# Linear attention regrouped around one matrix, phi read from PSUM by ScalarE alone, and transposes by DMA on the crossbar, in a four-layer attention and gated-MLP kernel

## The chip, the cores and the metric

The kernel runs on one core of one Trainium2 chip; the three later sessions used three chips. The metric is device time in microseconds (us) of one execution. Every execution told here was fast, with a granted TensorE clock of at least 0.99 of full speed as the mean of a run. A ratio is the mean time of one kernel's fast runs over the mean of the other's in the same rounds, so it is not quite the ratio of the medians quoted beside it.

Engine names: PE is TensorE, PEld its weight loads, DVE VectorE, ACT ScalarE, POOL GpSimd, and SP the engine that issues the DMAs.

## The reference

There are four layers: attention, MLP, attention, MLP. Each adds its result to `x`, which is 2048 x 1024, and normalises its input first.

```python
def _A_ref(x, wqkv, wo):                 # H = 32 heads of 32
    q, k, v = split(x @ wqkv)
    phi = lambda t: jnp.where(t > 0, t + 1, jnp.exp(t)) + 1e-6
    pq, pk = phi(q), phi(k)
    kv  = jnp.einsum("bhsd,bhse->bhde", pk, v)
    z   = jnp.einsum("bhsd->bhd", pk)
    num = jnp.einsum("bhqd,bhde->bhqe", pq, kv)
    den = jnp.einsum("bhqd,bhd->bhq", pq, z)[..., None] + 1e-6
    return merge_heads(num / den) @ wo
def _B_ref(x, w_gate, w_up, w_down):     # F = 3584
    return ((x @ w_gate) * (x @ w_up)) @ w_down
```

## The kernel before

The parts that matter, with cuts marked:

```python
def transpose_tile(src, dst):                    # 128 x 1024, on TensorE
    pt = psum.tile([P, KD, P], BF16, tag="tr", bufs=1, name="pt")
    for k in range(KD):
        nc.tensor.transpose(out=pt[:, k, :], in_=src[:, k * P:(k + 1) * P], identity=ident[:])
    nc.scalar.copy(out=dst, in_=pt[:])

def phi(ps, dst):                                # 128 x 512; VectorE reads PSUM too
    e = eb[phis[0] % 3]
    ...
    nc.scalar.activation(out=e, in_=ps[:], func=ACT.Exp)
    nc.vector.tensor_scalar(out=e, in0=e, scalar1=1.0, scalar2=1e-6, op0=ALU.min, op1=ALU.add)
    nc.vector.scalar_tensor_tensor(out=dst, in0=ps[:], scalar=1.0 + 1e-6, in1=e, op0=ALU.add, op1=ALU.max)

def kv_unit(t):                                  # phi(k)' [v, ones], 128 x 132 blocks
    ...
        for c in range(KD):
            nc.tensor.matmul(out=acc[0][:, c, 0:ZW], lhsT=pk[t % 4][:, c * P:(c + 1) * P],
                             rhs=vz[t % 4][:, c, :], ...)

def o_unit(t):                                   # phi(q) [kv, z], then a division
    ...
        for c in range(KD):
            nc.tensor.matmul(out=ps[:, c, 0:ZW], lhsT=pqT[g % 3][:, c, tl * P:(tl + 1) * P],
                             rhs=KVz[:, c, :], start=True, stop=True)
    ...                                          # divide, transpose the result, multiply by wo
```

Each attention projects K, V and Q, accumulates `kv` over the 16 row tiles, divides, transposes each output tile and multiplies it by `wo`. Per attention K, V, Q and out take 256 matmuls of 512 columns each; `kv` and `o` take 128 of 132 columns each. Normalised tiles and attention outputs are transposed on TensorE through a single PSUM buffer, 96 tiles of eight 128-column matmuls in all.

Of the kernel before, what the change touches and what calls it, by code (L numbers as in the profile page):

```python
# [9 lines left out]
ALU = mybir.AluOpType  # L10
BF16 = mybir.dt.bfloat16
# [3 lines left out]
def weave(main, fill, first, step):  # L15

    out, fill = [], list(fill)
    for i, u in enumerate(main):
        out.append(u)
        if fill and i >= first and (i - first) % step == 0:  # L20
            out.append(fill.pop(0))
    return out + fill
# [3 lines left out]
def kernel(  # L26
# [23 lines left out]
    MM = 3  # L50
    HC = P // 32
    ZW = P + HC
    ZS = NB // 2
# [3 lines left out]
    work = ctx.enter_context(tc.tile_pool(name="work", bufs=4))  # L57
# [3 lines left out]

    X = const.tile([P, NT, D], BF16, tag="X", name="X")
    xT = [const.tile([P, KD, G], BF16, tag=f"xT{i}", name=f"xT{i}") for i in range(NG)]
    Wr = [const.tile([P, KD, NB], BF16, tag=f"W{i}", name=f"W{i}") for i in range(4)]
    Dr = [const.tile([P, 4 * D], BF16, tag=f"D{i}", name=f"D{i}") for i in range(KF // 4)]
    H = const.tile([P, KF * G], BF16, tag="H", name="H")
    KVz = const.tile([P, KD, ZW], BF16, tag="KVz", name="KVz")

    hT = H[:].rearrange("p (f s) -> p f s", s=G)
    pk = [H[:, i * D:(i + 1) * D] for i in range(4)]  # L70
    o0 = 4 * D
    vz = [H[:, o0 + i * KD * ZW:o0 + (i + 1) * KD * ZW].rearrange("p (c f) -> p c f", f=ZW) for i in range(4)]
    o0 += 4 * KD * ZW
    onat = [H[:, o0 + i * D:o0 + (i + 1) * D] for i in range(4)]
    o0 += 4 * D
    eb = [H[:, o0 + i * NB:o0 + (i + 1) * NB] for i in range(3)]
    oT = [H[:, i * KD * G:(i + 1) * KD * G].rearrange("p (c s) -> p c s", s=G) for i in range(2)]
    wk = Wr[0:2]
    wv = Wr[2:4]
    wo = [Dr[i][:].rearrange("p (k n) -> p k n", n=NB) for i in (0, 1)]  # L80
    pqT = [Dr[i][:].rearrange("p (c s) -> p c s", s=G) for i in (2, 3, 4)]
    wq = [Dr[i][:].rearrange("p (k n) -> p k n", n=NB) for i in (5, 6)]
    wd = [Dr[f // 4][:, (f % 4) * D:(f % 4 + 1) * D] for f in range(KF)]
    ring = [Wr[0], Wr[1], Wr[2], Wr[3], xT[2], xT[3]]
# [9 lines left out]

    def load(dst, src):
        nc.sync.dma_start(out=dst, in_=src)

    def load_k(n):
        load(wk[n][:], wqkv_v[:, :, D + n * NB:D + (n + 1) * NB])

    def load_v(n):
        load(wv[n][:], wqkv_v[:, :, 2 * D + n * NB:2 * D + (n + 1) * NB])

    def load_q():
        for n in range(2):
            load(wq[n], wqkv_v[:, :, n * NB:(n + 1) * NB])

    def load_o():
        for n in range(2):
            load(wo[n], wo_v[:, :, n * NB:(n + 1) * NB])  # L110

    def load_gu(i):
        fb = i % FB
        load(ring[2 * i % 6][:], wg_v[:, :, fb * NB:(fb + 1) * NB])
        load(ring[(2 * i + 1) % 6][:], wu_v[:, :, fb * NB:(fb + 1) * NB])

    def load_d():
        for i in range(KF // 4):
            load(Dr[i][:].rearrange("p (f n) -> p f n", n=D), wd_v[:, 4 * i:4 * i + 4, :])

    load(X[:, 0, :], x_view[:, 0, :])
    load(X[:, 1, :], x_view[:, 1, :])
    for k in range(0, KD, 4):
        load(wk[0][:, k:k + 4, :], wqkv_v[:, k:k + 4, D:D + NB])
    load(X[:, 2, :], x_view[:, 2, :])
    load(X[:, 3, :], x_view[:, 3, :])
    load_k(1)
    load_v(0)
    load_v(1)
    for t in range(TPG, 2 * TPG):  # L130
        load(X[:, t, :], x_view[:, t, :])
    load_q()
    for t in range(2 * TPG, NT):
        load(X[:, t, :], x_view[:, t, :])
    load_o()


    ident = const.tile([P, P], BF16, tag="ident", name="ident")
    make_identity(nc, ident[:])
    mask = const.tile([P, ZW], F32, tag="mask", name="mask")  # L140
    nc.gpsimd.memset(mask[:], 0.0)
    for b in range(HC):
        nc.gpsimd.memset(mask[32 * b:32 * b + 32, 32 * b:32 * b + 32], 1.0)
        nc.gpsimd.memset(mask[32 * b:32 * b + 32, P + b:P + b + 1], 1.0)
    mhalf = const.tile([P, 1], F32, tag="mhalf", name="mhalf")
    nc.gpsimd.memset(mhalf[:], -0.5)
    warm = const.tile([P, 1], F32, tag="warm", name="warm")
    nc.scalar.activation(out=warm[:], in_=mhalf[:], func=ACT.Exp)

    nc.vector.memset(xT[3][:, 0, :], 0.0)  # L150
    zps = psum.tile([P, NB], F32, tag="mm", bufs=MM, name="zps")
    for i in range(16):
        nc.tensor.matmul(out=zps[:], lhsT=xT[3][:, 0, 0:P], rhs=xT[3][:, 0, :], start=True, stop=True)
# [4 lines left out]
    def ln_stats(t):  # L158
        st = small.tile([P, 2, 6], F32, tag="st", name="st")
        for c in range(2):  # L160
            nc.vector.bn_stats(out=st[:, c, :], in_=X[:, t, c * NB:(c + 1) * NB])  # L161
        mv = small.tile([P, 2], F32, tag="mv", bufs=2 * TPG, name="mv")
        nc.vector.bn_aggr(out=mv[:], in_=st[:])
        ve = small.tile([P, 1], F32, tag="ve", name="ve")
        nc.gpsimd.tensor_scalar(out=ve[:], in0=mv[:, 1:2], scalar1=1e-5, scalar2=None, op0=ALU.add)
        rstd = small.tile([P, 1], F32, tag="rstd", bufs=2 * TPG, name="rstd")
        nc.gpsimd.tensor_tensor(out=rstd[:], in0=ve[:], in1=mhalf[:], op=ALU.pow)
        stat[t] = (mv, rstd)

    xns = {}  # L170

    def ln_apply(t):
        mv, rstd = stat.pop(t)
        xn = work.tile([P, D], BF16, tag="xn", name="xn")
        nc.vector.tensor_scalar(out=xn[:], in0=X[:, t, :], scalar1=mv[:, 0:1], scalar2=rstd[:],
                                op0=ALU.subtract, op1=ALU.mult)
        xns[t] = xn

    def transpose_tile(src, dst):
        pt = psum.tile([P, KD, P], BF16, tag="tr", bufs=1, name="pt")  # L180
        for k in range(KD):
            nc.tensor.transpose(out=pt[:, k, :], in_=src[:, k * P:(k + 1) * P], identity=ident[:])  # L182
        nc.scalar.copy(out=dst, in_=pt[:])  # L183

    def tx(t, slot):

        def run():
            if t not in xns:
                ln_apply(t)
            tl = t % TPG  # L190
            transpose_tile(xns.pop(t), xT[slot][:, :, tl * P:(tl + 1) * P])
        return run

    def tx_group(g, slot):
        return [tx(g * TPG + tl, slot) for tl in range(TPG)]

    def mm_tile():
        return psum.tile([P, NB], F32, tag="mm", bufs=MM, name="ps")

    def kv_tile():  # L200
        return psum.tile([P, KD, ZS], F32, tag="kv", bufs=1, name="kv")

    phis = [0]

    def phi(ps, dst):

        e = eb[phis[0] % 3]
        phis[0] += 1
        nc.scalar.activation(out=e, in_=ps[:], func=ACT.Exp)  # L209
        nc.vector.tensor_scalar(out=e, in0=e, scalar1=1.0, scalar2=1e-6, op0=ALU.min, op1=ALU.add)  # L210
        nc.vector.scalar_tensor_tensor(out=dst, in0=ps[:], scalar=1.0 + 1e-6, in1=e, op0=ALU.add, op1=ALU.max)


    def k_unit(t, n):
        def run():
            ps = mm_tile()
            xt, tl = xT[t // TPG], t % TPG
            for k in range(KD):
                nc.tensor.matmul(out=ps[:], lhsT=xt[:, k, tl * P:(tl + 1) * P], rhs=wk[n][:, k, :],  # L219
                                 start=(k == 0), stop=(k == KD - 1))  # L220
            phi(ps, pk[t % 4][:, n * NB:(n + 1) * NB])
        return run

    def v_unit(t, n):
        def run():
            ps = mm_tile()
            xt, tl = xT[t // TPG], t % TPG
            for k in range(KD):
                nc.tensor.matmul(out=ps[:], lhsT=xt[:, k, tl * P:(tl + 1) * P], rhs=wv[n][:, k, :],  # L229
                                 start=(k == 0), stop=(k == KD - 1))  # L230
            c = n * (NB // P)
            nc.scalar.copy(out=vz[t % 4][:, c:c + NB // P, 0:P], in_=ps[:].rearrange("p (c f) -> p c f", f=P))
        return run

    acc = []

    def kv_unit(t):

        def run():
            if t == 0:  # L240
                acc[:] = [kv_tile()]
            for c in range(KD):
                nc.tensor.matmul(out=acc[0][:, c, 0:ZW], lhsT=pk[t % 4][:, c * P:(c + 1) * P],  # L243
                                 rhs=vz[t % 4][:, c, :], start=(t == 0 and c % 2 == 0),
                                 stop=(t == NT - 1), skip_group_check=True)
            if t == NT - 1:
                nc.vector.tensor_tensor(out=KVz[:], in0=acc[0][:, :, 0:ZW],
# [237 lines left out]
```

## Time and profile before

| what | before |
|---|---|
| time, median | 1730.41 us (4 runs) |
| profiled span | 1727.3 us |
| first attention, up to the first gate matmul | 277.8 us |
| second attention | 273.2 us |
| a group of four tiles in the MLP | 146.8 us, 145.0 where nothing is transposed in it |

The second attention is the time from the first gate matmul of the first MLP's last group to that of the second MLP, less one group.

The page's first part gives busy time, share of the span and number of instructions:

```profile
PE 1680.1 (97%) x8550; PEld 802.9 (46%) x8720; DVE 538.8 (31%) x963; ACT 341.3 (20%) x514; POOL 54.0 (3%) x152
```

TensorE bounds the kernel. Its busy share is not its efficiency, because matmuls overlap in the record: each of 512 columns is shown as 379 ns. The pace is read from the chain that ended last (start, duration, what, count):

```profile
388.75 10.74 PE ps L319 x49
399.54 10.74 PE ps L319 x49
```

From 388.75 to 399.54 is 10.79 us for about 50 matmuls, so 0.2158 us each. The 7424 wide matmuls that the layers need take 1602 us at that pace.

The rest lies in narrow matmuls and in waits. The groups of instructions (line, engine, operation, output and inputs, shapes, count, busy us and mean ns, idle us before them with the releasers) show the transposes:

```profile
L182 PE MATMUL pt<-ident,xn 128*128 128x128 bf16 x512 | 40.7, 225 | 15.3 <-DVE xn L175 8.8 <-ACT xT_72 L183 4.0 <-ACT xT_71 L183 1.8
L182 PE MATMUL pt<-ident,H 128*128 128x128 bf16 x256 | 19.5, 219 | 3.1 <-DVE H L272 3.0
```

A record is 0.22 us long, but eight of them start within 0.45 us, so TensorE moves on by 0.056 us for each. The list of waits (engine, line, released by what; us in total, times, longest us), line by line:

```profile
PE pt L182 <- DVE xn L175: 8.8, 5, 6.0
PE kv L267 <- DVE H L272: 7.4, 8, 1.6
PE ps L219 <- ACT xT_70 L183: 4.7, 4, 1.4
PE pt L182 <- ACT xT_72 L183: 4.0, 4, 1.1
PE pt L182 <- DVE H L272: 3.0, 2, 1.5
```

The longest one, 6.0 us, is at the start of the second attention. TensorE's timeline there (start, duration, line, operation, count, idle before and its releaser):

```profile
865.95 0.61 PE L182 MATMUL pt<-ident,xn 128*128 128x128 bf16 x8
...
874.32 1.04 PE L182 MATMUL pt<-ident,xn 128*128 128x128 bf16 x8 [6.05 <-DVE xn L175]
```

The stretch as a whole, from 3 us before the second attention (window and its length; busy us and instructions of PE, PEld, DVE, ACT and POOL; granted clock, DMA share, GB/s):

```profile
862.10:890.00 27.90, 17.23 (x96) 9.46 (x96) 12.28 (x26) 7.85 (x9) 4.52 (x14) 0.76 0.48 151
```

The clock averages 0.76 there. The Trainium skill, "TensorE: Matmul & The Clock Gate", Part 1, says that the gate goes back to half rate after an idle window of about 3.4 us. This trace agrees: eight transposes take 0.61 us before the wait of 6.05 us and 1.04 us after it, so the wait costs more than its length.

### The profile page before, as it was taken

The page shows a single profiled execution, that of the slowest core. Times are in us where ns is not written, and L with a number is a line of the kernel's source. Part 1 is how long each engine was busy: PE and PEld are TensorE (multiplying, and loading weights), DVE is VectorE, ACT ScalarE, POOL GpSimd, SP SyncE. Part 2 cuts the span into 40 slices and gives each one's busy share as a digit, 9 for nine tenths or more (in the row PEclk, how much of TensorE's full clock was granted, in tenths as well). Part 3 has the DMA queues.
Part 4 walks back from the last instruction along what each step waited for, and adds up shares of the span by engine and source line. Part 5 has one row for each costly group of instructions (what it writes and reads, how often), then busy time and mean ns, then how long its engine had stood idle before and what let it go on. Part 6 is the DMA issues. An engine that isn't in the chain of part 4 may idle for free.

```text
span 1727.3 us, 19979 instructions
## 1 busy us (share of the span) xinstructions
PE 1680.1 (97%) x8550; PEld 802.9 (46%) x8720; DVE 538.8 (31%) x963; ACT 341.3 (20%) x514; POOL 54.0 (3%) x152
## 2 busy tenths in 40 slices
PE   8999989999999999999979999899999999999999
PEld 4444544444444444444444445444444444444444
DVE  5443774211321321231332337642113213211111
ACT  3333312210210120021033333222102101200110
POOL 2000000000000000000110000000000000000000
PEclk9999999999999999999989999999999999999999
DMA  8001306440441243043030022064404423431400
GB/s 292 1 1 54 94 1 219 147 146 1 146 146 49 93 145 104 16 147 114 17 98 1 1 79 68 1 221 146 152 19 146 146 68 104 146 107 57 154 4 22
DMA packets 147529, 158.58 MB, mean 92 GB/s; under 512 B 3056, under 2 KB 138224, under 8 KB 147440
## 3 DMA queue, kind: packets, MB, share of 16 engines
q1 hardware_dynamic: 147440, 157.30, 28.0%
q8 instruction: 68, 1.11, 0.3%
q14 instruction: 21, 0.17, 0.0%
HBM read 153.09 MB, written 4.19 MB: 91 GB/s over the span
## 4 chain that ended last, share of the span: by engine, by line
PE 95%; DVE 3%; ACT 1%; issue 1%; DMA 0%; SPq 0%; DVEq 0%; ACTq 0%
PE ps L307 45%; PE ps L319 22%; PE ps L229 6%; PE ps L256 6%; PE ps L219 6%; PE ps L293 5%; PE pt L182 2%; DVE st L161 1%; PE kv L243 1%; PE kv L267 1%; DVE H L272 1%; DVE X L285 1%; DMA X<-in_A_x_dram 0%; ACT xT_70 L183 0%; ACT xT_72 L183 0%
## 5 line engine op out<-in xcount | busy, mean ns | idle before, releaser
L311 DVE TENSOR_TENSOR H<-gs,ps 128x512 bf16<-128x512 f32 x224 | 154.0, 688 | 583.6 <-PE ps L307 561.5
L310 ACT COPY gs<-ps 128x512 f32<-128x512 f32 x224 | 131.0, 585 | 870.5 <-PE ps L307 867.6
L319 PEld LDWEIGHTS <-H 128*128 128x128 bf16 x1792 | 175.3, 98 | 211.0
L285 DVE TENSOR_TENSOR X<-X,ps 128x512 bf16<-128x512 bf16 x128 | 87.4, 683 | 375.4 <-PE ps L319 331.3
L209 ACT ACTIVATE H<-ps 128x512 bf16<-128x512 f32 x128 | 76.4, 597 | 149.7 <-PE ps L256 71.0
L210 DVE TENSOR_SCALAR H<-H 128x512 bf16<-128x512 bf16 x128 | 37.3, 291 | 199.3 <-ACT H L209 199.3
L307 PEld LDWEIGHTS <-W_75 128*128 128x128 bf16 x640 | 62.6, 98 | 75.5
L307 PEld LDWEIGHTS <-W_74 128*128 128x128 bf16 x640 | 62.2, 98 | 75.4 <-issue 2.4
L307 PEld LDWEIGHTS <-xT_73 128*128 128x128 bf16 x576 | 56.4, 98 | 67.9
L307 PEld LDWEIGHTS <-W_77 128*128 128x128 bf16 x576 | 56.4, 98 | 68.0
L307 PEld LDWEIGHTS <-W_76 128*128 128x128 bf16 x576 | 56.0, 98 | 66.1
L307 PEld LDWEIGHTS <-xT_72 128*128 128x128 bf16 x576 | 55.9, 98 | 65.3
L161 DVE BATCH_NORM_STATS2 st<-X 128x6 f32<-128x512 bf16 x128 | 80.9, 673 | 4.7 <-DMA X<-in_A_x_dram 4.7
L307 PE MATMUL ps<-xT_70,W_74 128*128 128x512 bf16 x312 | 75.2, 379 | 2.7 <-ACT xT_70 L183 2.2
L307 PE MATMUL ps<-xT_71,W_76 128*128 128x512 bf16 x313 | 75.2, 379 | 0.4
L307 PE MATMUL ps<-xT_71,W_74 128*128 128x512 bf16 x312 | 75.2, 379 | 0.5
L307 PE MATMUL ps<-xT_70,xT_72 128*128 128x512 bf16 x312 | 75.2, 379 | 0.4
L307 PE MATMUL ps<-xT_71,W_75 128*128 128x512 bf16 x315 | 75.2, 379 | 0.2
L307 PE MATMUL ps<-xT_71,W_77 128*128 128x512 bf16 x315 | 75.0, 379 | 0.2
L307 PE MATMUL ps<-xT_70,W_75 128*128 128x512 bf16 x316 | 75.1, 379 | 0.1
L307 PE MATMUL ps<-xT_70,xT_73 128*128 128x512 bf16 x314 | 75.0, 379 | 0.2
L293 PEld LDWEIGHTS <-H 128*128 128x128 bf16 x512 | 48.2, 98 | 49.6
(93 smaller groups left out, 1895.9 us busy)
## 6 DMA issues: line engine op xcount, KB each, us to landing
W_74<-in_B_w_gate_dram SPq DMA_DIRECT2D x20, 1024.0 KB, 5.4
W_75<-in_B_w_up_dram SPq DMA_DIRECT2D x20, 1024.0 KB, 7.4
W_76<-in_B_w_gate_dram SPq DMA_DIRECT2D x18, 1024.0 KB, 5.3
W_77<-in_B_w_up_dram SPq DMA_DIRECT2D x18, 1024.0 KB, 7.1
xT_72<-in_B_w_gate_dram SPq DMA_DIRECT2D x18, 1024.0 KB, 5.3
xT_73<-in_B_w_up_dram SPq DMA_DIRECT2D x18, 1024.0 KB, 6.9
X<-in_A_x_dram SPq DMA_DIRECT2D x16, 256.0 KB, 7.9
out_dram<-X SPq DMA_DIRECT2D x32, 128.0 KB, 1.7
```

The lines of the kernel that those rows point to most:

```text
L161: nc.vector.bn_stats(out=st[:, c, :], in_=X[:, t, c * NB:(c + 1) * NB])
L209: nc.scalar.activation(out=e, in_=ps[:], func=ACT.Exp)
L210: nc.vector.tensor_scalar(out=e, in0=e, scalar1=1.0, scalar2=1e-6, op0=ALU.min, op1=ALU.add)
L219: nc.tensor.matmul(out=ps[:], lhsT=xt[:, k, tl * P:(tl + 1) * P], rhs=wk[n][:, k, :], start=(k == 0), stop=(k == KD - 1))
L229: nc.tensor.matmul(out=ps[:], lhsT=xt[:, k, tl * P:(tl + 1) * P], rhs=wv[n][:, k, :], start=(k == 0), stop=(k == KD - 1))
L256: nc.tensor.matmul(out=ps[:], lhsT=wq[n][:, k, cl * P:(cl + 1) * P], rhs=xT[g][:, k, :], start=(k == 0), stop=(k == KD - 1))
L285: nc.vector.tensor_tensor(out=X[:, t, n * NB:(n + 1) * NB], in0=X[:, t, n * NB:(n + 1) * NB], in1=ps[:], op=ALU.add)
L293: nc.tensor.matmul(out=ps[:], lhsT=oT[(t // TPG) % 2][:, c, tl * P:(tl + 1) * P], rhs=wo[n][:, c, :], start=(c == 0), stop=(c == KD - 1))
L307: nc.tensor.matmul(out=ps[:], lhsT=w[:, k, j * P:(j + 1) * P], rhs=xT[g % 2][:, k, :], start=(k == 0), stop=(k == KD - 1))
L310: nc.scalar.copy(out=gs[:], in_=gp[:])
L311: nc.vector.tensor_tensor(out=hT[:, f, :], in0=gs[:], in1=up[:], op=ALU.mult)
L319: nc.tensor.matmul(out=ps[:], lhsT=hT[:, f, tl * P:(tl + 1) * P], rhs=wd[f][:, n * NB:(n + 1) * NB], start=(f == 0), stop=(f == KF - 1))
```

## The change

The intent is to take work off TensorE that is not a wide matmul. Since `kv` is `phi(k)' v` and `v` is `xn Wv`, the kernel forms `G = xn' phi(k)` (1024 x 1024), then the blocks of `kv` from `Wv` and `G`, masks them, and multiplies by `Wo` once, giving one matrix `M`. Then the output is `(phi(q) / den) M`. V's projection goes and G's comes, both 256 wide matmuls. Row tiles are transposed by DMA on the crossbar. A unit of K, Q or G fills two PSUM banks, and phi is `relu + min(exp, 1)`: for phi, ScalarE alone reads PSUM.

```diff
-            nc.tensor.transpose(out=pt[:, k, :], in_=src[:, k * P:(k + 1) * P], identity=ident[:])
-        nc.scalar.copy(out=dst, in_=pt[:])
+    def turn(src, slot, tl):
+        nc.sync.dma_start_transpose(out=xT[slot][:, :, tl * P:(tl + 1) * P], in_=src)
...
+        nc.scalar.activation(out=e[:], in_=flat(ps), func=ACT.Exp, **sc)
+        nc.scalar.activation(out=dst, in_=flat(ps), func=ACT.Relu, **sc)
+        nc.vector.tensor_scalar(out=e[:], in0=e[:], scalar1=1.0, scalar2=EPS, op0=ALU.min, op1=ALU.add)
+        nc.vector.tensor_tensor(out=dst, in0=dst, in1=e[:], op=ALU.add)
...
+        def z_sum():                    # sum of phi(k) over partitions, split in two bf16 parts
+            ps = mm_tile()
+            for h in range(2):
+                both(ps, ones[:], zhl[:, h, :], h == 0, h == 1)
+            nc.scalar.copy(out=zacc, in_=flat(ps))
+        def g_unit(m):
...
+                for t in range(NT):
+                    both(ps, XN[:, t, m * P:(m + 1) * P], PK[:, t, :], t == 0, t == NT - 1)
+        def kv_unit(m):                 # 64 matmuls of 128 columns per attention
...
+        def m_unit(c):
...
+                both(ps, KVb[:, c, :], wo[c], True, True)
...
+        do([g[0], z_sum, g[1], kv[0]] + d(0) + [g[2], kv[1]] + d(1, 2) + [q[0], g[3], kv[2]] + d(3, 4))
...                                     # d: divide a tile of phi(q) by its denominator, turn it
+                if g == NG - 1 and not last:   # MLP, last group: next attention's tiles
+                    do([a_norm(s) for s in range(4 * tl, 4 * tl + 4) if s < 12])
```

The first four tiles of the program are still transposed on TensorE. Their normalisation is deferred: the tiles are only centred, and the scale goes into phi.

## The prediction

> **What bounds the kernel now.** TensorE. The page gives PE 97% busy of 1727.3 us, DVE 31%, ACT 20%; the chain that ended last is 95% PE; the granted clock is 0.996. In the MLP, 512-column matmuls follow one another every 10.79/50 = 0.2158 us (the chain's 388.75 to 399.54). Either kernel needs 7424 of them: 1602 us. The other 125 us can be won: 768 transposes (about 0.056 us each, 43 us), 512 kv/o matmuls of 132 columns (0.058 us, 30 us), and some 52 us of start, end and waits. By stretches: attention 0 to 274.3 and 862.1 to 1134.8 us; MLP groups of 146.8 us, of which 145.0 are 512-column work.
>
> **What the change does to TensorE.** Per attention K, Q and out stay at 256 wide matmuls; V (256) goes, G = xn' phi(k) (256) comes. kv and o (256 narrow) become 64 narrow; M = KV Wo adds 16 wide, the denominator sums 4. Of all transposes 32 remain. Gone: 73 us; added: 9 us narrow, 9 us wide: 55 us less work, nearly all on the critical path. Weight loads stay one per matmul, hidden (46% busy).
>
> **Waits.** Gained: the second attention's start (6.05 us waiting for xn, then copies; clock 0.97 there) should vanish, because 12 tiles are normalised and turned during the last down-projection. The kernel's start: no wait for rstd, full-width K for four tiles: some 6 us. Lost: (a) first attention, K/Q phase: per unit of 16 matmuls (3.45 us) DVE has phi (0.5 + 0.65 us), stats 1.3 + 0.2, 0.9 waiting for POOL's rstd, apply 0.5: 4.2 us. DVE falls behind; tiles 4 to 7 have little slack, so TensorE waits 3 to 6 us for their turns. (b) The last z additions (1.2 us each, after the 128x1024 f32 multiply's 1224 ns) and the split end after the first G unit: 5 us in the first attention, 3 in the second. (c) M: eight evictions of 1.0 to 1.2 us on two engines, behind the last phi: 3 us each. Elsewhere evictions of 1 to 2 us fit in 3.45.
>
> **Crossbar transposes.** This trace has none. The Trainium skill, "Advanced Engine Details and Errata", X-Bar Transpose (TRN2), expects them nearly as fast as ordinary transfers; a 256 KB tile is then, by estimate, 1 us of queue and 3 us to landing. The tightest place, tiles 8 to 15 of the first attention, stands about 5 us per tile in series.
>
> **Sum.** First attention 10 (start) + 229 + 15 = 254; second 229 + 6 = 235; MLP 8 x 145.1 = 1161; tail 3: 1653 us profiled. Timed runs were 4 us above the profile: 1657. With unforeseen waits: 1660 us, range 1643 to 1688. Chances: faster 0.94, same 0.04, slower 0.02.
>
> **What would show it.** MLP groups at 145 us; 32 PE transposes; attention stretches near 254 and 235 us; PE waits led by xT from DMA early in the first attention, by the z sums before the second G unit, and by M's evictions; transposes landing in under 5 us.
>
> **What would make it wrong.** Transposes of 8 us or more each in series: both attentions, and the turns queued behind 8 MB of weights before the first MLP group, would stall TensorE by tens of us. Relu and Exp not sharing a table: 1.3 us per reload (the one load in the trace), twice per unit. DVE slower on all-bf16 adds than assumed.

## More of the kernel before

The kernel before was run again in each session, and its medians there were 1729.8 to 1730.7 us, so a difference between kernels of different sessions is known to about 1 us.

TensorE stood still 15.3 + 3.1 = 18.4 us ahead of transposes, because their data was late or because the one PSUM buffer had not been copied out. By the releasers 8.8 + 3.0 = 11.8 us of it is for VectorE's data and nearly all the rest for ScalarE's copy; a second PSUM buffer was not tried.

## The result, and the profile after

| | before | after |
|---|---|---|
| time, median of 4 runs | 1730.41 us | 1658.87 us |
| ratio, 95% interval | | 0.9586 (0.9572 to 0.9599) |
| profiled span | 1727.3 us | 1657.2 us |
| first attention | 277.8 us | 257.9 us |
| second attention | 273.2 us | 235.7 us |
| MLP group | 146.8 us | 145.04 us |
| last MLP to the end | 589.1 us | 583.5 us |

The page's first part of the changed kernel:

```profile
PE 1627.2 (98%) x7512; PEld 744.8 (45%) x7663; DVE 607.9 (37%) x889; ACT 286.3 (17%) x384; POOL 54.0 (3%) x141
```

ScalarE is less busy, though it now reads every phi twice, because it no longer copies out transposed tiles (97 us before, 2.3 after) or V (37 us). VectorE has 69 us more.

TensorE's waits in the changed kernel:

```profile
PE ps L205 <- DVE W L256: 6.7, 2, 5.1
PE pt L344 <- DVE R L336: 3.1, 2, 2.8
PE ps L205 <- ACT PQ L211: 2.3, 2, 1.2
...
PE ps L205 <- DMA xT<-R: 0.7, 1, 0.7
PE ps L205 <- DVE W L257: 0.7, 2, 0.6
PE ps L205 <- DVE R L309: 0.6, 2, 0.3
PE ps L205 <- ACT R L311: 0.6, 2, 0.3
```

Waits for transposed tiles are all but gone: 0.7 us for a crossbar transfer (`DMA xT`). The largest wait left is for the split sums of phi(k) (`W`, lines 256 and 257). The second, 2.8 us of 3.1, is for the centring of tile 3 at the start. Those for `PQ` and `R` (lines 211, 309 and 311) are at M, and the clock falls there too: in the stretch 193 to 203 us it averages 0.83. TensorE's timeline around the first `z_sum` (start, duration, line, operation, count, idle before and its releaser):

```profile
99.12 7.32 PE L205 MATMUL ps<-R,R 128*128 128x512 bf16 x31
111.58 1.01 PE L205 MATMUL ps<-W,ones 128*128 128x512 bf16 x2 [5.14 <-DVE W L256]
112.74 1.01 PE L205 MATMUL ps<-W,ones 128*128 128x512 bf16 x2 [0.15 <-DVE W L257]
113.55 8.81 PE L205 MATMUL ps<-R,R 128*128 128x512 bf16 x32
122.19 0.61 PE L295 MATMUL kv<-GL,W 128*128 128x128 bf16 x8
122.64 7.07 PE L205 MATMUL ps<-R,R 128*128 128x512 bf16 x31
```

The first G unit ends, TensorE waits 5.14 us, and the next G unit takes 8.81 us in place of 7.07: the clock is slow again after the wait. Groups of VectorE that set its load:

```profile
L320 DVE TENSOR_TENSOR X<-X,ps 128x1024 bf16<-128x1024 bf16 x32 | 38.5, 1209 | 33.1 <-PE ps L205 30.9 <-remote 2.2
L252 DVE TENSOR_TENSOR GL<-GL,R 128x1024 f32<-128x1024 f32 x28 | 34.2, 1221 | 0.5
L195 DVE TENSOR_SCALAR R<-X,mv,rstd 128x1024 bf16<-128x1024 bf16 x64 | 33.7, 543 | 36.0 <-POOL rstd L190 36.0
L213 DVE TENSOR_TENSOR R<-R,e 128x1024 bf16<-128x1024 bf16 x32 | 22.1, 692 | 11.4 <-ACT R L211 10.1
```

An addition of two bf16 tiles in SBUF takes 692 ns; with one operand in PSUM, or in f32, it takes 1.21 to 1.22 us. The Trainium skill, "VectorE: DVE Perf Modes", The perf-mode tier table, gives `tensor_tensor` two speeds of just this kind, and the trace agrees. And the crossbar transfers, from the list of DMA issues (count, median us from issue to landing):

```profile
xT<-R SPq DMA_TRANSPOSE x60, 3.1
xT<-PQ SPq DMA_TRANSPOSE x32, 3.1
```

### The profile page after: what moved, and what is told of

Read it like the earlier page. It is cut to its first block, busy times and chain, and to the rows that moved or that the text cites. A ratio compares the mean times of both kernels' runs of the same rounds, so it can differ in the third digit from the quotient of the medians.

```text
span 1657.2 us, 17618 instructions
## 1 busy us (share of the span) xinstructions
PE 1627.2 (98%) x7512; PEld 744.8 (45%) x7663; DVE 607.9 (37%) x889; ACT 286.3 (17%) x384; POOL 54.0 (3%) x141
## 4 chain that ended last, share of the span: by engine, by line
PE 90%; DVE 7%; issue 1%; DMA 1%; POOL 1%; ACT 0%; SPq 0%; DVEq 0%; ACTq 0%
PE ps L437 46%; PE ps L205 42%; DVE GL L252 1%; DVE st L182 1%; PE ps L464 1%; DVE R L213 1%; DVE X L320 0%; DVE den L272 0%; DVE PQ L276 0%; PE kv L295 0%; POOL rstd L190 0%; DVE PQ L213 0%; DVE tmp L270 0%; DVE e L212 0%; DVE R L195 0%
## 5 line engine op out<-in xcount | busy, mean ns | idle before, releaser
L437 PE MATMUL ps<-xT,R 128*128 128x512 bf16 x2380 | 525.8, 379 | 2.8
L437 PEld LDWEIGHTS <-R 128*128 128x128 bf16 x2432 | 238.0, 98 | 287.0
L441 DVE TENSOR_TENSOR R<-gs,ps 128x512 bf16<-128x512 f32 x224 | 153.8, 687 | 533.6 <-ACT gs L440 533.6
L205 PEld LDWEIGHTS <-R 128*128 128x128 bf16 x2248 | 220.4, 98 | 266.6 <-issue 3.1
L437 PE MATMUL ps<-xT,W 128*128 128x512 bf16 x1133 | 250.6, 379 | 1.0
L205 PEld LDWEIGHTS <-xT 128*128 128x128 bf16 x1536 | 149.8, 98 | 184.2 <-issue 5.3
L205 PE MATMUL ps<-W,xT 128*128 128x512 bf16 x999 | 225.1, 380 | 4.5 <-ACT xT L345 1.7
L437 PEld LDWEIGHTS <-W 128*128 128x128 bf16 x1152 | 112.7, 98 | 135.9
L205 PE MATMUL ps<-W,R 128*128 128x512 bf16 x729 | 169.6, 379 | 0.7
L205 PE MATMUL ps<-R,R 128*128 128x512 bf16 x503 | 114.5, 383 | 0.6
L205 PE MATMUL ps<-PQ,R 128*128 128x512 bf16 x484 | 111.5, 379 | 0.6
L210 ACT ACTIVATE e<-ps 128x1024 bf16<-128x1024 f32 x56 | 57.4, 1024 | 152.1 <-PE ps L205 150.6
L205 PE MATMUL ps<-xT,R 128*128 128x512 bf16 x243 | 58.2, 379 | 0.3
L320 DVE TENSOR_TENSOR X<-X,ps 128x1024 bf16<-128x1024 bf16 x32 | 38.5, 1209 | 33.1 <-PE ps L205 30.9
```

What stands on the lines that cost most here:

```text
L205: nc.tensor.matmul(out=ps[:, n, :], lhsT=lhsT, rhs=rhs[:, n * NB:(n + 1) * NB], start=start, stop=stop)
L210: nc.scalar.activation(out=e[:], in_=flat(ps), func=ACT.Exp, **sc)
L320: nc.vector.tensor_tensor(out=X[:, t, :], in0=X[:, t, :], in1=flat(ps), op=ALU.add)
L437: nc.tensor.matmul(out=ps[:, n, :], lhsT=w[:, k, j * P:(j + 1) * P], rhs=xT[g % 2][:, k, :], start=(k == 0), stop=(k == KD - 1))
L441: nc.vector.tensor_tensor(out=hT[:, f, :], in0=gs[:], in1=ps[:, 1, :], op=ALU.mult)
```

## The experiments

The total was as predicted, but how it is shared out had not been tested. The theory: TensorE's own work is what went, 41 us of it transposes. Rivals: the regrouping makes the gain, or waits do. The first three experiments form a square with the two kernels and add a control. The next two ask whether VectorE and the crossbar have slack. The last four try to win back the waits seen above.

### before_xbar: the crossbar alone

```diff
-            transpose_tile(xns.pop(t), xT[slot][:, :, tl * P:(tl + 1) * P])
+            src, dst = xns.pop(t), xT[slot][:, :, tl * P:(tl + 1) * P]
+            if pe_first and t < TPG:          # the program's first four tiles
+                transpose_tile(src, dst)
+            else:
+                nc.sync.dma_start_transpose(out=dst, in_=src[:])
...
-            transpose_tile(onat[tl], oT[(t // TPG) % 2][:, :, tl * P:(tl + 1) * P])
+            nc.sync.dma_start_transpose(out=oT[(t // TPG) % 2][:, :, tl * P:(tl + 1) * P], in_=onat[tl])
```

> The kernel before with its transposes, all but the first four tiles', on the DMA crossbar; nothing else changed. Theory (the gain is TensorE work removed, and the transposes are its larger half): 736 transposes x 0.056 us = 41 us less, about 6 to 9 us less at the start of the second attention, where TensorE waits for xn, and 2 to 4 us lost twice at the start of an MLP, where the last turned tile now lands 3 us after it is issued. About 1686 us, ratio 0.974. Rival 1 (the reassociation brings most of it): 1715 us or more. Rival 2 (with weights in the same queue the turned tiles come late and stall TensorE): slower than 1730 us.

Measured: 1669.18 us, ratio 0.9649 (0.9634 to 0.9663). That is 60.6 us less than the 1729.82 us of before in the same session, not the 44 expected: the expectation failed. Three of its waits, to be held against before:

```profile
PE kv L272 <- DVE H L277: 8.5, 10, 2.1
...
PE ps L312 <- DMA xT<-xn: 2.0, 2, 1.0
...
PE pt L183 <- DVE xn L176: 0.6, 2, 0.3
```

The waits ahead of transposes, 18.4 us in before, are down to 0.6 us, and the MLP's first units wait only 2.0 us in total for their turned tiles. The second attention starts at 837.35 us here; the stretch that lies around its start as 862.1 to 890 did in before is at full clock, with 127 matmuls of which 16 are narrow, where before had 96 with 48 narrow transposes among them:

```profile
834.39:862.29 27.90, 25.69 (x127) 11.89 (x129) 16.94 (x36) 6.90 (x12) 4.54 (x14) 1.00 0.63 154
```

So the crossbar alone brings 60.6 us; the whole change brought about 71.5.

### before_xbar_dummy: the transposes' work without their waits

```diff
+    def dummy():
+        pt = psum.tile([P, KD, P], BF16, tag="tr", bufs=1, name="pt")
+        for k in range(KD):
+            nc.tensor.transpose(out=pt[:, k, :], in_=ident[:], identity=ident[:])
...
                 nc.sync.dma_start_transpose(out=dst, in_=src[:])
+                dummy()                       # and the same in to_unit
```

> Before_xbar (1669 us) with the eight narrow transposes of each tile put back on TensorE at their old places, but reading a constant and read by nobody: TensorE's work of the transposes without their waits. Theory (of the crossbar's 60.6 us, 736 x 0.056 = 41 us are TensorE time and the rest the waits for VectorE's data and ScalarE's copy, 18.3 us in the list of waits of before): 1708 to 1712 us. Rival (the transposes' own time on TensorE is larger than 0.056 us each, and the waits hide elsewhere): 1720 to 1730 us.

Measured: 1706.00 us, ratio 0.9860 (0.9843 to 0.9876). This is 2 us below the expected range. The narrow matmuls cost 1706.0 - 1669.2 = 36.8 us net, or 0.050 us each. (At 0.056 us each they are 41 us of work, as expected, but they fill some waits: by the sums of the lists, TensorE waits 20.1 us in before_xbar and 15.9 here.) The other 23.8 us of the crossbar's 60.6 are what the real transposes cost beyond that: standing still for data and for the copy, and the slow clock after it. They lie in the attentions, 7.4 us in the first and 15.5 in the second; an MLP group takes 146.8 us as in before. TensorE's listed waits are 35.0 us in before, so 19.1 us of the 23.8 are waits. The slow clock after the 6.05 us wait makes some 3.7 us more. That is an estimate: from 874.32 to 887.04 us stand 32 transposes and 16 wide matmuls, which at the full-clock pace of the same trace (1.71 us for a tile that waits for the copy, 0.2158 us for a wide matmul) would end 3.7 us earlier.

### after_pe: the change without the crossbar

```diff
     def turn(src, slot, tl):
-        nc.sync.dma_start_transpose(out=xT[slot][:, :, tl * P:(tl + 1) * P], in_=src)
+        pend.append([age, src, slot, tl])
+    def tick(all=False):                      # called before each unit
...                                            # transposes on TensorE, two units later
+            for k in range(KD):
+                nc.tensor.transpose(out=pt[:, k, :], in_=src[:, k * P:(k + 1) * P], identity=ident[:])
+            nc.scalar.copy(out=xT[slot][:, :, tl * P:(tl + 1) * P], in_=pt[:])
```

A few weight loads and output units had to move with it, so that no tile is overwritten before it is transposed.

> The changed kernel with every crossbar transpose put back on TensorE (placed two units after the data is made, copied out by ScalarE); the reassociation, two-bank units and phi stay. Theory: 736 transposes x 0.056 us = 41 us more, and 0 to 10 us of waits for xn or for the copies: 1700 to 1712 us, still faster than before. Rival (crossbar alone makes the gain): 1725 us or more. If the two parts are independent, its loss against the changed kernel equals the gain of the crossbar in the kernel before, within the waits.

Measured: 1733.06 us, ratio 1.0020 (1.0000 to 1.0039): no faster than before. TensorE's largest waits, in a profile of the slowest of the four runs (1738.2 us):

```profile
PE pt L210 <- DVE R L195: 21.2, 15, 2.5
PE pt L210 <- DVE PQ L288: 4.2, 2, 2.1
PE ps L217 <- ACT PQ L223: 3.9, 4, 1.4
```

The expectation, 1700 to 1712 us, failed much as the first did: the work was counted, but the waits were put at 0 to 10 us, and those for VectorE's data ahead of transposes alone are over 25. The placement of the transposes was not tuned (even an MLP group takes 147.9 us, 1.1 more than in before), and they share the three PSUM buffers of the units, so 74 us is what they cost in this order of work, not what they must cost.

### after_oldphi: phi as before

```diff
-        nc.scalar.activation(out=dst, in_=flat(ps), func=ACT.Relu, **sc)
-        nc.vector.tensor_tensor(out=dst, in0=dst, in1=e[:], op=ALU.add)
+        # where no scale is needed (56 of 64 units):
+            nc.vector.scalar_tensor_tensor(out=dst, in0=flat(ps), scalar=1.0 + EPS, in1=e[:],
+                                           op0=ALU.add, op1=ALU.max)
```

> The changed kernel with phi as before (VectorE adds and takes the maximum straight from PSUM) for 56 of the 64 units; the eight with a scale keep Relu. Theory: one VectorE instruction of 1.22 us replaces one of 0.69, so VectorE goes from 4.1 to 4.65 us per unit of 3.45 us while it normalises tiles in the first attention, and PSUM is now held until it is done: 6 to 12 us slower there, nothing in the second, 1665 to 1671 us. Rival (ScalarE's two passes of 1.0 us are the tighter limit, or phi is off the path): same within 2 us, or faster.

Measured: 1665.63 us, ratio to before 0.9624 (0.9608 to 0.9640), so 6.8 us slower than the changed kernel's 1658.87 us. The first attention is 264.7 us (257.9 in the changed kernel), the second 235.9 (235.7). TensorE now waits for VectorE to let go of PSUM (line 217):

```profile
PE ps L205 <- DVE PQ L217: 4.7, 6, 1.0
PE ps L205 <- DVE R L217: 4.1, 6, 1.0
```

All but 0.3 us of these waits lie in the first attention. Where VectorE normalises tiles beside phi, TensorE's units now come 4.65 us apart, VectorE's time for one unit in the expectation:

```profile
66.72 3.61 PE L205 MATMUL ps<-W,xT 128*128 128x512 bf16 x16 [1.03 <-DVE R L217]
71.37 3.61 PE L205 MATMUL ps<-W,xT 128*128 128x512 bf16 x16 [1.03 <-DVE PQ L217]
```

This is as expected: phi matters only where VectorE also normalises tiles or, right after, adds up z.

### after_turn2: every crossbar transpose twice

```diff
+        nc.sync.dma_start_transpose(out=KVb[:], in_=src)
         nc.sync.dma_start_transpose(out=xT[slot][:, :, tl * P:(tl + 1) * P], in_=src)
```

> The changed kernel with every crossbar transpose issued twice, the extra one first and into a tile that is not in use then (right result). Theory: the crossbar has slack. A tile lands 3.1 us after issue and one is asked for every 4.1 us at most, so 92 more of them cost at most 5 us, by tiles that land later at the start of the first attention: 1659 to 1664 us. Rival (transposes or the queue are near their limit): 20 us or more slower.

Measured: 1658.18 us, ratio 0.9590 (0.9573 to 0.9607): the same as the changed kernel. The transfers land nearly as fast as before (3.1 us):

```profile
KVb<-R SPq DMA_TRANSPOSE x60, 3.2
xT<-R SPq DMA_TRANSPOSE x60, 3.2
```

The crossbar and the queue have room for twice the transposes. The danger that the prediction named, transposes that land late in series, is far off. But the equal time is a balance and does not show that the extra ones are free: TensorE's waits for turned tiles rise from 0.7 to 2.6 us, and it waits 2.0 us for the tile that the extra ones write, while the wait at the first `z_sum` falls from 5.14 to 3.08 us and the mean clock is 0.999 in place of 0.995.

### after_zlate: the denominator's sum one unit later

```diff
-        do([g[0], z_sum, g[1], kv[0]] + ...
+        do([g[0], g[1], z_sum, kv[0]] + ...
```

> The changed kernel with the denominator's sum over partitions placed after the second G unit in place of the first. Theory: TensorE's waits for the split z sums go (5.1 + 0.15 us in the first attention, 1.6 + 0.6 us in the second), and with them the slower clock after the first of them (a G unit took 8.8 us there, 7.07 elsewhere): 9 us less, 1650 us. Rival (the divisions, now 7 us later, only move the wait to their turned tiles or to phi's slots): 0 to 3 us less.

Measured: 1646.03 us, ratio to before 0.9511 (0.9498 to 0.9524): 12.8 us less than the changed kernel. The first attention is 248.4 us, the second 232.2. The timeline at the same place:

```profile
98.85 14.22 PE L205 MATMUL ps<-R,R 128*128 128x512 bf16 x63
112.91 1.03 PE L205 MATMUL ps<-W,ones 128*128 128x512 bf16 x4
113.77 0.61 PE L295 MATMUL kv<-GL,W 128*128 128x128 bf16 x8
114.22 7.07 PE L205 MATMUL ps<-R,R 128*128 128x512 bf16 x31
```

No wait and no slow unit are left here, and nothing came back later. The listed waits were 7.4 us in both attentions together, and the slow clock after the 5.14 us wait cost 2.7 us more (1.7 in the G unit, 1.0 in the sum itself). Most of the rest is clock at M, where the work and the waits (1.16, 0.31 and 0.33 us) are the same in both kernels. Eight of M's matmuls in the first attention, in the changed kernel and in this one:

```profile
198.85 3.47 PE L205 MATMUL ps<-PQ,KVb 128*128 128x512 bf16 x8 [0.33 <-DVE R L309]
190.42 2.28 PE L205 MATMUL ps<-PQ,KVb 128*128 128x512 bf16 x8 [0.33 <-DVE R L309]
```

From here to the next unit the changed kernel takes 0.9 us longer, and 1.0 in the second attention: about 1.9 of the 12.8 us came with the change and were not aimed at. Why the same waits slow the clock in one kernel and not in the other was not tested.

### after_start: tile 3 prepared earlier

```diff
             ln_stats(2)
             centre(2)
+            ln_stats(3)
+            centre(3)
             k_part(0, 6, 8)
...
-            ln_stats(3)
-            centre(3)
             k_part(2, 0, 4)
```

> The changed kernel with tile 3's statistics and centring placed before the first phi in VectorE's order. Theory: TensorE's wait of 2.8 us for tile 3's centring at 21.9 us, behind the first two phi on VectorE, and the slow clock around it go: 3 to 5 us less, 1654 to 1656 us. Rival (tile 3's load or the weights come too late for it to matter; phi and the copies of tile 2 are held up in turn): within 1 us of the changed kernel.

Measured: 1653.62 us, ratio 0.9555 (0.9542 to 0.9568), 5.2 us less than the changed kernel. The first 30 us, in the changed kernel:

```profile
0.00:30.00 30.00, 23.22 (x110) 10.36 (x113) 12.99 (x27) 10.72 (x13) 5.72 (x21) 0.94 0.79 280
```

And with tile 3 earlier:

```profile
0.00:30.00 30.00, 25.27 (x124) 11.65 (x127) 14.93 (x32) 12.46 (x15) 5.74 (x21) 1.00 0.79 280
```

The clock stays at 1.00 and 14 more matmuls fit. The gain is more clock than wait: all of TensorE's listed waits fall only from 18.6 to 16.7 us, since those for weights grow by 1.1, and M of the first attention also ran at full clock in this kernel, worth some 0.9 us.

### after_all: both, and another order at M

```diff
-        do([q[6], kv[7], q[7]])
-        do([m_unit(c) for c in range(KD)])
+        m = [m_unit(c) for c in range(KD)]
+        do([kv[7], q[6]] + m[:2] + [q[7]] + m[2:])
```

> After_zlate, after_start and one more: the last kv unit before the last two Q units, and two of M's units between these. Theory: the first two add up, 12 to 14 us; M's reordering changes little, minus 1 to plus 3 us, since the last kv unit now waits for the copy of G: 1645 to 1650 us. Rival: the gains don't add, 1650 us or more.

Measured: 1646.51 us, ratio 0.9515 (0.9502 to 0.9528), no better than after_zlate. The second attention, where the start plays no part, is 234.5 us against 232.2: the new order at M loses 2.3 us there. TensorE now waits for the copy of G ahead of the last kv unit, and twice as often for phi at M:

```profile
PE ps L205 <- ACT PQ L211: 4.7, 4, 1.2
PE kv L295 <- ACT GL L285: 2.3, 2, 1.2
```

### after_zstart: both, without the order at M

> The denominator's sum after the second G unit and tile 3 prepared earlier, without the reordering of M of after_all. Theory (the two gains add, 12.8 and 5.2 us less some overlap; M's reordering cost 2.3 us in each attention): 1641 to 1643 us, first attention near 244 us, second at 232 us. Rival (the start's gain is eaten by VectorE's lag in the first attention): 1646 us, as after_zlate.

Measured: 1641.59 us, ratio to before 0.9489 (0.9475 to 0.9503), correct, and faster than both kernels: 17.3 us below the changed one. The first attention is 243.8 us, the second 232.2. The two gains add up within 1 us (12.8 + 5.2 = 18.0).

## Why the prediction was right, and where it was not

**The time.** 1658.87 us measured, 1660 predicted. By stretches: first attention 254 predicted, 257.9 measured; second 235 and 235.7; MLP group 145.1 and 145.04; tail 3 and 583.5 - 4 x 145.04 = 3.3. The MLP groups of before_xbar are 145.04 us too, so nothing beside the transposes gained time in the MLP, two-bank units included. The sum came out although the gain was shared out wrongly (next point), because it counted what the new kernel does and waits for, not what goes. That it is 1 us off is partly luck: 1653 us were summed for the profile against 1657.2 measured, 3 us were then added for unforeseen waits and 4 for a gap that is 1.8 us (below), and in the first attention the start was too low by 5.5 us and (a) too high by 2 to 5. None of the three dangers named came: transposes land in 3.1 us, the trace shows one table load as before, and a bf16 addition takes 0.69 us (0.65 assumed).

**The share of the transposes was mis-sized.** The prediction put the gain as "55 us less work, nearly all on the critical path", 41 us of it transposes, and counted as waits gained only the second attention's start and the kernel's start. The experiments show 60.6 us for the crossbar alone, of which 36.8 us are work and 23.8 are not. Of these the prediction named the second attention's start, but gave a size only for its one wait, 6.05 us. The term that was too small stood in the profile: 18.4 us of idle time ahead of the transposes in all, and a clock of 0.76 around the longest wait. The rest of the change then gave 1669.2 - 1658.9 = 10.3 us on top of the crossbar, and without it, in the order of work tried, nothing (1733.06 against 1729.82 us).

**(a) VectorE falling behind.** The rate was right: 4.1 us per unit in the trace, 4.2 predicted. The wait was not: 0.75 us for turned tiles, not 3 to 6. Tile 4's transfer was issued at 38.5 us, and with 3.1 us to land it was there before its K unit started near 43 us; only the last of the four came late. That VectorE is at its limit there was shown by after_oldphi: with 0.5 us more per phi TensorE kept VectorE's pace, 4.65 us per unit, and 6.8 us were lost. In the changed kernel ScalarE frees the PSUM of a unit, and VectorE's lag did not stop TensorE before the z sums: there VectorE is busy without a break from 84 us up to the split that ends the wait of 5.14 us.

**(b) The z sums.** 5 and 3 us predicted; the list shows 5.1 and 1.6 us for the first half and 0.7 us for the second half of the split. The slow clock after the first wait was not foreseen. The order was a choice, not a need: after_zlate won back 12.8 us, some 1.9 of them at M.

**(c) M.** 3 us each predicted; 1.2 + 0.3 + 0.3 = 1.8 us of waits each measured, and 0.9 and 1.0 us of slow clock after them, so nearly 3 in all; the clock was not foreseen. The one reordering tried lost time.

**The start.** Predicted 10 us beyond the work of four K tiles. By the trace, ScalarE takes up tile 3's result at 29.3 us, and four K units are 13.8 us, so it was about 15.5 us, with 2.8 us of waiting for tile 3's centring and a slow clock; after_start removed 5.2 us.

**Two slips.** The stretches of before were cut one unit early: its first attention ends at 277.8 us, not 274.3. And "timed runs were 4 us above the profile" compared different executions: in one and the same run the time is 1.8 us above the span (1729.17 and 1727.4 us, for one). The slips did not decide the result.

**What stays open.** How much of the remaining 10.3 us is the regrouping and how much the new orders of work was not separated by a run, beyond phi's 6.8 us. An account from the traces, which is not a test, closes for after_zlate: its gap to before_xbar is 23.2 us. The regrouping's TensorE work by the prediction's own counts is 14 us less (30 us gone, 9 us wide and 7 us narrow added; the other 2 us narrow are the 32 transposes, which before_xbar has too). TensorE's listed waits are 9.4 us less (20.1 and 10.7), the wait for the divided tile (`kv L272`, 8.5 us) among them.

## What to carry to other kernels

Work that TensorE does for other engines in between its own costs its own time and also every moment that it stands there for its data: here 36.8 and 23.8 us. So read the idle column of a group together with its busy time before costing its removal, and test with a dummy of the same work on ready data. On TensorE look also at the clock after the waits: it was slow after 6.05 and 5.14 us, but three short waits at M slowed it in one kernel and not in another, so a gain of 1 or 2 us can be the clock and not the change. After a large gain, look at the list of waits again: two changes of a few lines in the order of work gave another 17.3 us here.

## What the Trainium skill lacked or had wrong

- "Advanced Engine Details and Errata", X-Bar Transpose (TRN2), gives a bandwidth and "DMA: Bandwidth & Descriptors", DMA Transpose (X-bar), the constraints; neither gives the time of one tile within SBUF. ("VectorE: DVE Perf Modes", The three transpose paths, has one for 128 x 128 only.) Here a 128 x 1024 bf16 tile took 3.1 us (median of 60 and of 32) from issue to landing beside weight loads, and 3.2 us with twice as many transposes.
- "TensorE: Matmul & The Clock Gate", Part 4: PE-mode transpose, gives about 275 ns for one in a kernel. The records here are 219 to 225 ns long, but transposes among matmuls follow one another every 0.056 us, and on ready data 736 of them cost 0.050 us each, net of the waits that they filled. Part 4 does not tell this pace, which is the one to count with.
- The same page, Part 1, names an idle window of about 3.4 us for the return to half rate, and under "A second HAM failure mode: psum-queue depth-cycling" it says that frequent short idles between groups of matmuls make the clock swing too, but not how short or how many. In the changed kernel the clock was also slow after one wait of 2.81 us (0.72 on average from 21 to 27 us) and, at M, after waits of 1.16, 0.31 and 0.33 us (0.83 from 193 to 203 us). In after_zlate the same waits at M left it at 1.00.
